# The first two weight blocks loaded and cast by column halves, and the remaining queries of batches 0 and 1 loaded ahead of batch 2

## The chip, the cores and the metric

The kernel runs on one core of one Trainium2 chip. The metric is the device time of one execution in microseconds (us). A profiled execution also gives a span, from the first to the last instruction of the program; it was about 1.8 us shorter than the time of the same execution.

In the profile the engines are PE (TensorE matmuls), PEld (its weight loads), DVE (VectorE), ACT (ScalarE), POOL (GpSimd) and SP (SyncE, whose queue issues nearly all DMAs here). The text says VectorE for DVE.

## The reference

Linear attention on 8 batches of 8 heads, 576 positions and 64 channels, followed by a two-layer network on all 4,608 rows:

```python
q_s = exp(q - max(q, -1)) / sum(..., -1)        # softmax over the channels
k_s = exp(k - max(k, 2))  / sum(..., 2)         # softmax over the positions
kv  = einsum('bhsd,bhse->bhde', k_s, v)
x   = einsum('bhsd,bhde->bhse', q_s, kv)        # -> (4608, 512)
h   = x @ w_in                                  # 512 -> 2048
g   = h * sigmoid(beta * h)
out = g @ w_out                                 # 2048 -> 512
```

## The kernel before

The rows are cut into nine slabs of 512. Slab t, for t below 8, holds the first 512 positions of batch t. The last 64 positions of each batch, the *remaining* queries, are gathered for the ninth slab. They go in pairs of batches: loaded into `QRF`, exponentiated into `EQR`, normalized, transposed by a DMA into `QTR`, and multiplied on PE by the `KVD` of their two batches.

A slab has a first pass (`x @ w_in`, then Silu on ACT) and a second (`g @ w_out`). PE interleaves the attention work of the next batch with these. The kernel gives each engine its instructions in the order of the program. The helper `add(engine, instruction, r=, w=)` derives waits from what is read and written.

Three places matter. The first is the start, where the first weight group `(c = 0)` is loaded in four blocks `m` of 128 rows by 512 columns and cast to bf16. The second is the queue order of batch loads. The third is the product with `QTR` in slab 1.

```python
def load_qrem(b):                  # two loads, rows of 64 float32 = 256 bytes
    for h in range(2):
        a = bass.AP(qt_h, (b + h) * H * S * D + SM * D, [[D, SR], [S * D, H], [1, D]])
        ...                        # SP: dma_start(QRF[i][64 * h:64 * h + 64, :, :], a)

def load(b):                       # all of it on the SP queue, in this order
    load_main("qf", qt_h, QF, b)
    load_k(b)
    load_v(b)
    if b % 2:
        load_qrem(b - 1)
# ... cut ...
def load_win(c, m=0, nm=NM):       # a block: 128 rows of 512 columns, 2 KB each
    a = bass.AP(win_h, m * 128 * DFF + 512 * c, [[DFF, 128], [128 * DFF, nm], [1, 512]])
    add(SP, lambda e: e.dma_start(STAGE[c][:, m:m + nm, :], a), w=SKEY[c][m:m + nm], ...)
# ... cut: start of slab 0 ...
out_now(0, 0, 0, ACTE)
cast_win(0, 0, DVE)                # block 0 of the first group
kv_mm(0, 2, 7, 0, D + 1)
ksum_inv(0, 7, 2, 1, D, 1)
kvd(0, 2, 7, 0)
cast_win(0, 1, DVE)                # block 1; blocks 2 and 3 are cast by POOL
out_now(0, 1, 6, ACTE)
at = by_m(0, 0, 4)                 # first-pass matmuls of columns 0:512, block by block
kv_mm(0, 3, 1, 0, D + 1)
at(0)
# ... cut: end of slab 0 ...
if t == 0:
    load(2)
    load_qrem(0)
    ...
    store(0)
    load(3)                        # contains load_qrem(2)
    continue
# ... slab 1, between the passes ...
if t == 1:
    nb = [2, 3]
    exp_qr(0)                      # ACT: EQR <- exp(QRF)
    norm_rem(0)                    # VectorE: sums, reciprocals, scaling
    tr_dma(0)                      # SP: QTR <- EQR, a transposing DMA
for b in nb:
    exp_q(b)
    ...
# the second pass of slab 1 contains the products with QTR, then batch 2's attention
```

The products with `QTR` cannot simply be put later on PE. They read the `KVD` of batches 0 and 1, and the next thing that PE does for the attention is to make the `KVD` of batch 2 in the same buffer.

The softmax here doesn't subtract the row's maximum and nothing guards it: scores larger than these inputs give would overflow.

Of the kernel before, what the change touches and what calls it, by code (L numbers as in the profile page):

```python
# [17 lines left out]
DFF = 2048  # L18
NF = DFF // 128
NM = DM // 128  # L20
# [136 lines left out]
def bass_efficient_attn_shen__then__act_swish_beta_kernel(  # L157
# [12 lines left out]
    with ExitStack() as es:  # L170
# [24 lines left out]
        WIN = sb("WIN", [128, NM, DFF], BF16)  # L195
# [20 lines left out]
        add = P.add  # L216
# [55 lines left out]
        def load_v(b, split=1, cs=None):  # L272
            load_pairs("vf", vt_h, VF, b, split, cs)

        def load(b):
# [5 lines that stand above are left out]
# [65 lines left out]
        def cast_v(b, hp, eng=POOL, part=None):  # L346
            i = b % 2
            j0, n = ((0, NG), (0, 5), (5, 4))[0 if part is None else part + 1]
            o = bass.AP(VB[i], (hp * NG + j0) * VW, [[NHP * NG * VW, 128], [VW, n], [1, 64]])
            a = bass.AP(VF[i], hp * KW + j0 * D, [[NHP * KW, 128], [64, n], [1, 64]])  # L350
            add(eng, lambda e: (e.copy if eng == ACTE else e.tensor_copy)(o, a),  # L351
                r=[("vf", i, hp), ("vone", i)],
                w=[("vb", i, hp, h) for h in ((0, 1) if part is None else (part,))])
# [211 lines left out]
        def cast_win(c, m, eng):  # L565
            add(eng, lambda e: e.tensor_copy(WIN[:, m, 512 * c:512 * c + 512], STAGE[c][:, m, :]),  # L566
                r=[SKEY[c][m]], w=[("win", c, m)])

        KB = 2

        def turn_beta():
# [36 lines left out]
        go(t_steps(0, (1,), (4,)))  # L608
        ksum(0, 0, KB)
        load_v(0, 4)  # L610
        for c in range(4):
            for m in range(0, NM, 1 if c < 2 else 2):
                load_win(c, m, 1 if c < 2 else 2)
        cast_v(0, 0)
        cast_v(0, 1)
        cast_v(0, 2, ACTE)
        cast_v(0, 3)
        cast_win(0, 2, POOL)
        cast_win(0, 3, POOL)
        cast_win(1, 0, POOL)  # L620
# [13 lines left out]
        def pass1_mm(t, f, m, bk):  # L634
            x = XT8 if t == 8 else XT[t % 2]
            rd = [("xt8", p_) for p_ in range(4)] if t == 8 else [("xt", t % 2, m)]
            n = 2 if f < 8 else 4
            l = bass.AP(WIN, m * DFF + 128 * (f // n * n) + f % n, [[NM * DFF, 128], [n, 128]])
            mm(PS[bk][:, :], l, x[:, m, :], m == 0, m == NM - 1,
               r=rd + [("win", f // 4, m)], w=[("ps", bk)], bk=bk)  # L640
            if m == NM - 1:
                add(ACTE, lambda e: e.activation(GT[:, f, :], PS[bk][:, :], ACT.Silu,  # L642
                                                 scale=BETA[:, f:f + 1]),
                    r=[("ps", bk), "beta"], w=[("gt", f)], bank=[bk])
# [17 lines left out]

        FIRST = (16, 5)
        out_now(0, 0, 0, ACTE)
        cast_win(0, 0, DVE)
        kv_mm(0, 2, 7, 0, D + 1)
        ksum_inv(0, 7, 2, 1, D, 1)
        kvd(0, 2, 7, 0)
        cast_win(0, 1, DVE)
        out_now(0, 1, 6, ACTE)  # L670
        at = by_m(0, 0, 4)
        kv_mm(0, 3, 1, 0, D + 1)
# [36 lines left out]
        def o2_evac(t, u, bk, eng=DVE):  # L709
            add(eng, lambda e: (e.copy if eng == ACTE else e.tensor_copy)(  # L710
                O2S[t % 2][:, u, :], PS[bk][:, :]),
                r=[("ps", bk)], w=[("o2", t % 2, u)], bank=[bk])
# [41 lines left out]
        for t in range(NSLAB):  # L754
            todo = []
            if t == 0:
                def kv1():
                    kv_mm(1, 1, 0, 1, D + 1)
                    ksum_inv(1, 0, 0, 2, D, VW)
                    kvd(1, 0, 0, 0, 2)  # L760

                def evacs():
                    o2_evac(0, 0, 3, DVE)
                    exp_kh(1, 3, 1, 1)
                    exp_kh(1, 3, 1, 0)
                    o2_evac(0, 1, 4, ACTE)

                todo = [(107, lambda: go(t_steps(1, (0, 1), (1,), ACTE))),
                        (112, lambda: go(t_steps(1, (2, 3), (2,), ACTE))),
                        (112.1, lambda: (scale_wout(14, 2), exp_kh(1, 2, 1, 0), exp_kh(1, 2, 1, 1))),  # L770
                        (115, lambda: kv_mm(1, 0, 0, 0, D + 1)), (117, kv1),
                        (122, lambda: out_now(1, 0, 7, DVE)),
                        (123, lambda: out_now(1, 1, 1, ACTE)), (124.5, evacs),
                        (126, lambda: go(kv_steps(1, (2,), (0,))))]
            elif t == 1:
                todo = spread(outr_steps(1), 101.5, 103) + attn_late(2)
            elif t < 7:
                todo = attn(t + 1)
            todo = sorted(todo, key=lambda x: -x[0])
            slot = [0]  # L780

            def tick():
                slot[0] += 1
                while todo and todo[-1][0] <= slot[0]:
                    todo.pop()[1]()

            if 2 <= t < 7:
                for hp in (0, 2):
                    norm_main(t + 1, hp, 2)
                    t_dma(t + 1, hp, 2)  # L790
                if t % 2 == 0:
                    norm_rem(t // 2)
                    tr_dma(t // 2)
                if t == 2:
                    load(5)
            elif t == 1:
                for hp in range(NHP):
                    cast_v(2, hp)
            if t < 2:
                slot[0] = NM * FIRST[t]  # L800
            for f in range(FIRST[t] if t < 2 else 0, NF):
                pass1_tile(t, f, tick)
            if t == 0:
                load(2)
                load_qrem(0)
                scale_wout(0)
                scale_wout(4)
                exp_q(1, 0, 2)
                norm_main(1, 0, 1)
                scale_wout(8)  # L810
                norm_main(1, 1, 1, POOL)
                exp_q(1, 2, 2)
                exp_kh(1, 0, 2, 0)
                exp_kh(1, 0, 2, 1)
                norm_main(1, 2, 1, POOL)
                norm_main(1, 3, 1)
                scale_wout(12, 2)
                for hp in range(NHP):
                    cast_v(1, hp, POOL if hp else ACTE)
                pass2_group(0, (0, 1, 2, 3), (3, 4, 5, 6), tick)  # L820
                while todo:
                    todo.pop()[1]()
                at = by_m(1, 0, FIRST[1])
                o2_evac(0, 2, 5, ACTE)
                add(ACTE, lambda e: e.activation(DUMMY[:, 2:3], WARM[:, 0:1], ACT.Silu),
                    r=["warm"], w=["dummy"])
                at(0, 0, 3)
                out_now(1, 2, 7, DVE)
                at(1, 0, 3)
                go(kv_steps(1, (3,), (0,)))  # L830
                at(0, 3)
                at(1, 3)
                out_now(1, 3, 7, DVE)
                at(2)
                at(3)
                o2_evac(0, 3, 6, DVE)
                store(0)
                load(3)
                continue
            nb = [t + 2] if t + 2 < B else []  # L840
            if t == 1:
                nb = [2, 3]
                exp_qr(0)
                norm_rem(0)
                tr_dma(0)
            for b in nb:
                exp_q(b)
                if b == 2:
                    for hp in range(2):
                        norm_main(2, hp, 1, POOL)  # L850
                    t_dma(2, 0, 2)
                if b % 2 == 1:
                    exp_qr(b // 2)
                exp_k(b, step=2)
                if b > 3:
                    for hp in range(NHP):
                        cast_v(b, hp)
                if b + 2 < B and t > 1:
                    load(b + 2)
            for u in range(4):  # L860
                if (t, u) == (8, 3):
                    last_tile(u, ((0, 384), (384, 512)), (OB[orot[0] % 2], MB[0]))
                    continue
                pass2_group(t, (u,), (OB[orot[0] % 2],), tick)
                orot[0] += 1
                if t == 1 and u == 0:
                    for hp in range(2, 4):
                        norm_main(2, hp, 1, POOL if hp == 2 else DVE)
                    t_dma(2, 2, 2)
                    for hp in range(NHP):  # L870
                        cast_v(3, hp)
                    load(4)
            while todo:
                todo.pop()[1]()
            if t < 8:
                store(t)
# [30 lines left out]
```

## Time and profile before

| quantity | value |
|---|---|
| time, median of the 6 runs beside the changed kernel | 285.24 us (284.43 to 285.64) |
| span of the profiled execution | 283.1 us |
| PE busy | 275.2 us, 97% |
| first weight matmul starts | 13.77 us |
| product with `QTR` starts | 68.08 us |

These are the page's span, its first busy rows, the granted clock and the busy share of the DMA engines in 40 slices of 7.08 us (9 is 90% or more), and the two rows of the chain that ended last.

```profile
span 283.1 us, 3884 instructions
...
PE 275.2 (97%) x1559; PEld 136.0 (48%) x1589; DVE 117.3 (41%) x218; ACT 178.6 (63%) x243; POOL 38.6 (14%) x57
...
PEclk9999999999999999999999999999999999999999
DMA  7999999998998998217980033002500030012022
...
PE 90%; ACT 4%; DMA 3%; issue 1%; DVE 1%; SPq 0%; ACTq 0%
PE PS L366 89%; ACT EK L317 2%; DMA KF<-in_k_dram 2%; DMA QTR<-EQR 2%; ACT L322 0%; SPq L249 0%; PE PS L364 0%; ACT GT L642 0%; DVE QRS L340 0%; DVE EQR L343 0%; ACT VB L351 0%; ACT EQR L322 0%; ACT XT L530 0%; ACT O2S L710 0%; DVE O2S L731 0%
```

PE is the bound, and at full clock. No faster load, cast or exponential helps unless PE was waiting for it. PE busy is a coarse guide here, because the page models where pipelined matmuls end. The better reading is the distance from one matmul's start to the next one's: a 512-column matmul takes 215 to 216 ns. I looked in the trace for distances beyond that. Excesses of about 216 ns, one in about every 50 records, I took for missing records. What remains after 13 us is small: 0.11 us at 13.77, 0.17 us at 16.98, about four of 0.1 us or somewhat more between 39 and 53, and 0.73 us at 68.08.

The lines below are of the timeline of PE: start, time from there to the end of the group, engine, line, operation, output and inputs, shape, count, and in brackets idle time before it with what ended it. First the start of the first pass:

```profile
13.77 1.02 PE L366 MATMUL PS<-XT,WIN 128*128 128x512 bf16 x4
14.63 0.38 PE L366 MATMUL PS<-QT,KVD 128*128 128x512 bf16 x1
```

Four weight matmuls start at 13.77 and the next product follows at 14.63 without a hole. And at the remaining queries:

```profile
59.15 8.36 PE L366 MATMUL PS<-WOUT,GT 128*128 128x512 bf16 x37
68.08 0.26 PE L366 MATMUL PS<-QTR,KVD 128*128 128x64 bf16 x3 [0.57 <-DMA QTR<-EQR]
```

PE has run through 37 matmuls of the second pass and then waits for `QTR`. The last start before the wait was at 67.135 us, so PE could have gone on at 67.35; it went on at 68.08.

The queue and ACT tell where `QTR` came from. The first answer is the timeline of SP, where the second number is how long the issue occupied SP; the second is that of ACT.

```profile
33.42 0.43 SPq L249 DMA_DIRECT2D QF<-in_q_dram  x1
...
41.74 4.48 SPq L266 DMA_DIRECT2D QRF<-in_q_dram  x2
...
49.30 0.43 SPq L249 DMA_DIRECT2D QF<-in_q_dram  x1
...
54.13 5.35 SPq L266 DMA_DIRECT2D QRF<-in_q_dram  x2
63.69 1.29 SPq L456 DMA_TRANSPOSE QTR<-EQR  x1
```

```profile
46.19 1.28 ACT L825 ACT_TABLE_LOAD   x1
...
48.87 5.99 ACT L642 ACTIVATE GT<-PS,BETA 128x512 bf16<-128x512 f32 x10 [1.18 <-PE PS L366]
...
61.35 0.63 ACT L322 ACTIVATE EQR<-QRF 128x512 bf16<-128x512 f32 x1
```

The remaining queries of batches 0 and 1 are issued at 41.74, behind batch 2 (its q is the issue at 33.42), and landed, by the trace, at 54.0 and 54.4. Batch 3 follows from 49.30 on, with its own remaining queries last (54.13). ACT, busy with Silu, exponentiates them only at 61.35, and the transpose is issued at 63.69. It landed at 68.03.

### The profile page before, as it was taken

What the parts mean: (1) busy time and instruction counts of PE and PEld (TensorE: products, weight loads), DVE (VectorE), ACT (ScalarE), POOL (GpSimd) and SP (SyncE); (2) the same over time, 40 slices, a digit from 0 to 9 for tenths busy, and PEclk for the clock granted to TensorE, in tenths of its full rate; (3) what the DMA queues carried; (4) which work ended last, traced back from release to release, by engine and by line L of the source; (5) the groups of instructions that cost most, each with busy time, mean ns of one, the idle gap of its engine ahead of it and who ended that gap; (6) DMA issues with size and microseconds to landing.
All of it is one profiled execution on the core that took longest, in us unless ns stands there. A gap on an engine that the chain in (4) does not pass through costs nothing.

```text
span 283.1 us, 3884 instructions
## 1 busy us (share of the span) xinstructions
PE 275.2 (97%) x1559; PEld 136.0 (48%) x1589; DVE 117.3 (41%) x218; ACT 178.6 (63%) x243; POOL 38.6 (14%) x57
## 2 busy tenths in 40 slices
PE   7899999999999999999999999999999999999995
PEld 3545454444455445544554445444544444444443
DVE  4864886029781348124841473055705300110012
ACT  5968687999968926795579636892660076017500
POOL 6522041308021032100130000000000000000000
PEclk9999999999999999999999999999999999999999
DMA  7999999998998998217980033002500030012022
GB/s 243 375 391 400 389 387 378 347 382 138 336 322 251 362 365 285 39 35 252 375 102 1 0 150 74 2 1 100 141 2 0 9 141 0 0 54 96 0 74 74
DMA packets 41466, 50.07 MB, mean 177 GB/s; under 512 B 20324, under 2 KB 28772, under 8 KB 40296
## 3 DMA queue, kind: packets, MB, share of 16 engines
q1 hardware_dynamic: 40496, 48.77, 53.7%
q10 hardware_dynamic: 952, 1.06, 1.1%
q8 instruction: 12, 0.20, 0.3%
q14 instruction: 6, 0.05, 0.0%
HBM read 36.71 MB, written 9.44 MB: 163 GB/s over the span
## 4 chain that ended last, share of the span: by engine, by line
PE 90%; ACT 4%; DMA 3%; issue 1%; DVE 1%; SPq 0%; ACTq 0%
PE PS L366 89%; ACT EK L317 2%; DMA KF<-in_k_dram 2%; DMA QTR<-EQR 2%; ACT L322 0%; SPq L249 0%; PE PS L364 0%; ACT GT L642 0%; DVE QRS L340 0%; DVE EQR L343 0%; ACT VB L351 0%; ACT EQR L322 0%; ACT XT L530 0%; ACT O2S L710 0%; DVE O2S L731 0%
## 5 line engine op out<-in xcount | busy, mean ns | idle before, releaser
L642 ACT ACTIVATE GT<-PS,BETA 128x512 bf16<-128x512 f32 x144 | 96.6, 689 | 79.0 <-PE PS L366 79.0
L366 PE MATMUL PS<-WOUT,GT 128*128 128x512 bf16 (+2 forms) x579 | 131.4, 373 | 0.7 <-issue 0.2
L366 PE MATMUL PS<-XT,WIN 128*128 128x512 bf16 x561 | 131.2, 379 | 0.5
L366 PEld LDWEIGHTS PS<-XT,WIN 128*128 128x128 bf16 x576 | 60.1, 106 | 59.3 <-POOL WIN L566 0.5
L366 PEld LDWEIGHTS PS<-WOUT,GT 128*128 128x128 bf16 x592 | 55.3, 98 | 62.0 <-DVE O2S L710 0.2
L710 DVE COPY O2S<-PS 128x512 f32<-128x512 f32 x33 | 22.7, 687 | 107.7 <-PE PS L366 107.7
L366 PE MATMUL PS<-VB,EK 128*128 128x65 bf16 (+2 forms) x306 | 35.8, 191 | 1.2 <-ACT VB L351 0.7
L351 POOL CAST VB<-VF 128x576 bf16<-128x576 f32 x30 | 22.7, 757 | 76.5 <-DMA VF<-in_v_dram 47.1
L307 ACT ACTIVATE EK<-KF 64x1152 bf16<-64x1152 f32 x24 | 27.8, 1157 | 0.4
L366 PEld LDWEIGHTS PS<-VB,EK 128*128 128x128 bf16 x306 | 22.0, 98 | 8.1 <-ACT VB L351 0.8
L332 DVE TENSOR_REDUCE QS<-EQ 128x8 f32<-128x512 bf16 (+1 forms) x22 | 20.1, 913 | 3.1 <-ACT EQ L295 2.9
L441 DVE CAST XT<-PS 128x512 bf16<-128x512 f32 x24 | 16.4, 690 | 10.9 <-PE PS L366 10.9
L295 ACT ACTIVATE EQ<-QF 128x512 bf16<-128x512 f32 x32 | 17.9, 619 | 3.0 <-DMA QF<-in_q_dram 2.8
L334 DVE TENSOR_TENSOR EQ<-EQ,QI 128x1024 bf16<-128x1024 bf16 (+1 forms) x15 | 16.9, 1128 | 0.5
L366 PE MATMUL PS<-QT,KVD 128*128 128x512 bf16 x30 | 11.4, 379 | 0.0
L317 ACT ACTIVATE EK<-KF 64x576 bf16<-64x576 f32 (+1 forms) x12 | 9.9, 839 | 1.8 <-DMA KF<-in_k_dram 1.7
L334 POOL TENSOR_TENSOR EQ<-EQ,QI 128x512 bf16<-128x512 bf16 x7 | 7.3, 1042 | 18.5 <-DVE QI L333 18.2
L403 DVE TENSOR_TENSOR KVD<-PS,RC 64x64 bf16<-64x64 f32 (+2 forms) x28 | 8.6, 308 | 1.3 <-PE PS L364 0.5
L340 DVE TENSOR_REDUCE QRS<-EQR 128x8 f32<-128x512 bf16 x4 | 2.7, 678 | 13.2 <-ACT EQR L322 13.2
L366 PE MATMUL PS<-XT 128*128 128x512 f32 x10 | 6.7, 801 | 1.5 <-DVE XT L219 1.5
L642 ACT ACT_TABLE_LOAD x5 | 6.4, 1283 | 0.1
L295 ACT ACT_TABLE_LOAD x5 | 6.4, 1283 | 0.1
(52 smaller groups left out, 77.5 us busy)
## 6 DMA issues: line engine op xcount, KB each, us to landing
out_dram<-O2S SPq DMA_DIRECT2D x8, 1024.0 KB, 4.6
KF<-in_k_dram SPq DMA_DIRECT2D x6, 1152.0 KB, 8.2
VF<-in_v_dram SPq DMA_DIRECT2D x6, 1152.0 KB, 11.4
QF<-in_q_dram SPq DMA_DIRECT2D x6, 1024.0 KB, 6.8
KF<-in_k_dram SPq DMA_DIRECT2D x8, 288.0 KB, 8.1
VF<-in_v_dram SPq DMA_DIRECT2D x8, 288.0 KB, 8.7
WST<-in_moe_w_in_dram SPq DMA_DIRECT2D x8, 256.0 KB, 7.8
O2S<-in_moe_w_in_dram SPq DMA_DIRECT2D x4, 512.0 KB, 11.9
```

Of the source, the lines that this page charges most:

```text
L295: add(ACTE, lambda e, o=o, a=a: e.activation(o, a, ACT.Exp), r=[("qf", i, hp)], w=[("eq", i, hp)])
L307: add(ACTE, lambda e, o=o, a=a: e.activation(o, a, ACT.Exp), r=[("kf", i, h) for h in hps], w=[("ek", i, h, e_) for h in hps])
L317: add(ACTE, lambda e: e.activation(o, a, ACT.Exp), r=[("kf", i, h) for h in hps], w=[("ek", i, h, e_) for h in hps])
L332: add(DVE, lambda e: e.tensor_reduce(s_, a, AX.X, ALU.add), r=ks, w=[("qs", i, hp0)])
L334: add(eng, lambda e: e.tensor_tensor(a, a, vb, ALU.mult), r=ks + [("qi", i, hp0)], w=ks)
L340: add(DVE, lambda e: e.tensor_reduce(QRS[:, :], EQR[i][:, :, :], AX.X, ALU.add), r=[("eqr", i)], w=["qrs"])
L351: add(eng, lambda e: (e.copy if eng == ACTE else e.tensor_copy)(o, a), r=[("vf", i, hp), ("vone", i)], w=[("vb", i, hp, h) for h in ((0, 1 ...
L366: add(PE, lambda e: e.matmul(o, l, r_, start=start, stop=stop), r=r, w=w, bank=[bk])
L403: add(DVE, lambda e, o=o, a=a, s_=s_: e.tensor_tensor(o, a, s_, ALU.mult), r=[("ps", bk)] + [("rc", i, h) for h in hps], w=[("kvd", i, h, ...
L441: add(eng, lambda e: (e.copy if eng == ACTE else e.tensor_copy)(XT[i][:, hp, :], PS[bk][:, :]), r=[("ps", bk)], w=[("xt", i, hp)], bank=[bk])
L642: add(ACTE, lambda e: e.activation(GT[:, f, :], PS[bk][:, :], ACT.Silu, scale=BETA[:, f:f + 1]), r=[("ps", bk), "beta"], w=[("gt", f)], ba ...
L710: add(eng, lambda e: (e.copy if eng == ACTE else e.tensor_copy)(O2S[t % 2][:, u, :], PS[bk][:, :]), r=[("ps", bk)], w=[("o2", t % 2, u)], ...
```

## The change

The change has two parts. The *halves*: blocks 0 and 1 of the first group are loaded together, 256 columns at a time, so that one load of 256 KB, as large as a block's load before, brings half of both (a *half load*). VectorE casts the left halves and POOL the right ones, to shorten the way to the first matmuls and to relieve VectorE. The *queries*: the remaining queries of batches 0 and 1 are loaded ahead of batch 2. Their exponential goes before ACT's Silu work, and their normalization and transpose into the end of slab 0, so that PE need not wait for `QTR`.

```diff
+        def load_wh(h):
+            a = bass.AP(win_h, 256 * h, [[DFF, 128], [128 * DFF, 2], [1, 256]])
+            add(SP, lambda e: e.dma_start(STAGE[0][:, 0:2, 256 * h:256 * h + 256], a),
+                w=[("wsth", h)], slot=f"winh{h}")
+
+        def cast_wh(m, h, eng):
+            c = slice(256 * h, 256 * h + 256)
+            add(eng, lambda e: e.tensor_copy(WIN[:, m, c], STAGE[0][:, m, c]),
+                r=[("wsth", h), SKEY[0][m]], w=[("winh", m, h)])
 ...
+        load_wh(0)
+        load_wh(1)
         for c in range(4):
-            for m in range(0, NM, 1 if c < 2 else 2):
+            for m in range(0 if c else 2, NM, 1 if c < 2 else 2):
                 load_win(c, m, 1 if c < 2 else 2)
 ...
         cast_v(0, 3)
+        cast_wh(0, 1, POOL)
+        cast_wh(1, 1, POOL)
         cast_win(0, 2, POOL)
 ...
-               r=rd + [("win", f // 4, m)], w=[("ps", bk)], bk=bk)
+               r=rd + [("winh", m, f // 2) if f < 4 and m < 2 else ("win", f // 4, m)],
+               w=[("ps", bk)], bk=bk)
 ...
-        cast_win(0, 0, DVE)
+        cast_wh(0, 0, DVE)
 ...
-        cast_win(0, 1, DVE)
+        cast_wh(1, 0, DVE)
 ...
             if t == 0:
+                load_qrem(0)
                 load(2)
-                load_qrem(0)
 ...
                 o2_evac(0, 2, 5, ACTE)
+                exp_qr(0)
 ...
                 o2_evac(0, 3, 6, DVE)
+                norm_rem(0)
                 store(0)
                 load(3)
+                tr_dma(0)
                 continue
 ...
             if t == 1:
                 nb = [2, 3]
-                exp_qr(0)
-                norm_rem(0)
-                tr_dma(0)
```

## The prediction

> **What bounds the kernel.** The page's busy table: PE 275.2 of 283.1 us (97%), granted clock 1.0. The chain of waits runs 89% through PE's matmul line. PE waits for k, v and softmax until 12.87 us and hardly stops after 13.8, so only idle PE time can be won. From the timeline's starts (a 512-column matmul every 215 ns) I find after 13 us, besides an excess of 215 ns about every 50 records, taken for a missing record: 0.11 us at 13.77 (first weight matmul; its block landed at 13.17, VectorE cast it 13.20 to 13.63), 0.17 us at 16.98 (fourth x tile, evacuated until 16.83), about four of 0.1 us between 39 and 53, and 0.73 us at 68.08, where the remaining-query product waits for the transposed load QTR (waits view: 1.1 us for the weight load, 0.6 for the matmul). The change aims at the first and the last: at most 0.9 us.
>
> **Part 1, the halves.** Same bytes; rows of 1 KB instead of 2 KB. Packets took about 46 ns per 1,024 B at the start and 75 ns per 2,048 B in the weight loads: 512 KB should take 1.5 instead of 1.2 us over 16 engines, an estimate. The Trainium skill, "DMA: Bandwidth & Descriptors", section "Why small descriptors are slow (HBM only)", names a fixed cost per packet; the trace agrees (22 against 27 B/ns). So the first half lands near 13.3, the second near 14.0, later weights up to 0.3 us later. VectorE casts halves (estimate 0.25 us, from 0.42 for a whole); POOL must cast the others (estimate 0.35 us, from 0.61 to 0.80) before columns 256 to 511 can be used, which PE wants at 14.1. I expect the 0.11 us stall to go and one of 0.1 to 0.4 us, on POOL, before the third matmul: net -0.1 to +0.3, centre +0.1. The 0.17 us at 16.98 stays.
>
> **Part 2, remaining queries.** They landed at 54.0 and 54.4 behind batch 2; now near 45.5. Their exp (0.61 us, ACT) then runs near 46.2, before the Silu table load, after which ACT waited 1.18 us for PE: free, unless they land after 47. Sums, scaling and transpose issue, at 62.0 to 63.7 before, come at about 49 on VectorE and 59.5 on the queue. The transpose took 4.35 us to land at 68.03 (median 3.0): batch 3's own last piece landed at 67.47, and it still stands behind that batch. I expect QTR at 67.0 to 67.9, against a need at 67.35: saves 0.2 to 0.73 us, centre 0.45. Lighter ACT and VectorE in slab 1's second pass gain nothing.
>
> **Sum.** +0.1 - 0.45 = -0.35 us; the runs before spread 0.9 us, their median at the top. Predicted 284.8 us, 8 in 10 within 283.9 to 285.6. Faster by over 2%: 0.5%; within 2%: 99%; slower: 0.5%.
>
> **What shows it.** Right: the remaining exp near 46 without a DMA wait, slab 1's first Silu still near 48.9; QTR wait under 0.5 us; a PE weight-load wait on POOL's cast at 14; span 282.3 to 283.2. Part 2 wrong if the transpose lands at 68 or later (queue order decides, not issue time). Part 1 wrong if weight matmuls start clearly before 13.6 or PE runs through.
>
> **What would break it.** Remaining queries landing after 47: ACT holds back slab 1's Silu, PE loses up to 1 us. 256-byte rows slowing batch 1's last k and v (needed near 45.7, landed 43.9). A stall that timed runs have and the profile does not.

## The result

| | before | after |
|---|---|---|
| time, median of 6 | 285.24 us (284.43 to 285.64) | 285.24 us (284.78 to 286.22) |
| span of the profiled execution | 283.1 us | 283.1 us |
| first and third weight matmul start | 13.77, 14.20 us | 13.76, 14.53 us |
| remaining queries land | 54.0, 54.4 us | 44.7, 45.4 us |
| their exponential starts | 61.35 us | 46.30 us |
| transpose issued | 63.69 us | 59.11 us |
| `QTR` lands | 68.03 us | 67.98 us |
| PE ready for `QTR` | 67.35 us | 67.58 us |
| product with `QTR` starts | 68.08 us | 68.03 us |

The ratio of the changed kernel's time to that of before is 1.0011, with a 95% interval of 0.9987 to 1.0034: the same. "PE ready" is worked out: the start of the last matmul before the product with `QTR`, plus 216 ns.

The page of the changed kernel, the same parts as before:

```profile
span 283.1 us, 3887 instructions
...
PE 275.7 (97%) x1559; PEld 136.1 (48%) x1589; DVE 117.6 (42%) x218; ACT 178.7 (63%) x243; POOL 39.1 (14%) x59
...
PE 89%; DMA 6%; SPq 2%; ACT 1%; issue 1%; POOL 0%; DVE 0%
PE PS L366 89%; DMA QTR<-EQR 3%; DMA WST<-in_moe_w_in_dram 3%; SPq L259 1%; ACT EK L317 0%; SPq L249 0%; PE PS L364 0%; ACT GT L657 0%; ACT XT L530 0%; ACT O2S L725 0%; SPq L571 0%; POOL WIN L576 0%; DVE O2S L746 0%
```

The span is the same. The chain now passes through the transpose for 3% of the span, which is its 8.9 us from issue to landing: it was issued early and landed late.

The start of the first pass, first PE, then POOL:

```profile
13.76 0.59 PE L366 MATMUL PS<-XT,WIN 128*128 128x512 bf16 x2
14.53 0.61 PE L366 MATMUL PS<-XT,WIN 128*128 128x512 bf16 x2 [0.17 <-POOL WIN L576]
14.97 0.38 PE L366 MATMUL PS<-QT,KVD 128*128 128x512 bf16 x1
```

```profile
14.07 0.86 POOL L576 CAST WIN<-WST 128x256 bf16<-128x256 f32 x2 [0.80 <-DMA WST<-in_moe_w_in_dram]
```

PE starts two weight matmuls at 13.76 and then waits for POOL. From start to start the hole is 0.33 us, although the bracket counts 0.17, because the second matmul still counts as running. So the product that started at 14.63 before starts at 14.97 now. The right halves landed at 14.02, POOL's first cast ran 0.40 us from 14.07, and PE went on at 14.53.

At the remaining queries:

```profile
59.38 8.37 PE L366 MATMUL PS<-WOUT,GT 128*128 128x512 bf16 x37
68.03 0.26 PE L366 MATMUL PS<-QTR,KVD 128*128 128x64 bf16 x3 [0.29 <-DMA QTR<-EQR]
```

PE comes about 0.23 us later than before (59.38 against 59.15), waits less (0.29 against 0.57 in brackets, 0.45 against 0.73 from start to start) and goes on at nearly the same moment. The queue and ACT:

```profile
33.05 4.24 SPq L266 DMA_DIRECT2D QRF<-in_q_dram  x2
37.33 2.68 SPq L249 DMA_DIRECT2D QF<-in_q_dram  x1
...
52.18 6.88 SPq L266 DMA_DIRECT2D QRF<-in_q_dram  x2
59.11 4.69 SPq L456 DMA_TRANSPOSE QTR<-EQR  x1
```

```profile
46.30 0.63 ACT L322 ACTIVATE EQR<-QRF 128x512 bf16<-128x512 f32 x1
46.95 1.28 ACT L841 ACT_TABLE_LOAD   x1
...
49.09 5.99 ACT L657 ACTIVATE GT<-PS,BETA 128x512 bf16<-128x512 f32 x10 [0.64 <-PE PS L366]
```

Everything in front of the transpose moved forward as meant. The queries (33.05) are issued ahead of batch 2 (37.33), ACT exponentiates them without waiting for a load, and the first Silu of slab 1 still starts when PE delivers (49.09). Yet the transpose (59.11) stands behind all of batch 3 in the queue, its remaining queries (52.18) last, and lands 0.56 us after the last piece of it (67.42), as it did before (67.47 and 68.03).

### The profile page after: what moved, and what is told of

It reads as the page before. It is cut to its first block, busy times and chain, and to the rows that moved or that the text cites. A ratio compares the mean times of both kernels' runs of the same rounds, so it can differ in the third digit from the quotient of the medians.

```text
span 283.1 us, 3887 instructions
## 1 busy us (share of the span) xinstructions
PE 275.7 (97%) x1559; PEld 136.1 (48%) x1589; DVE 117.6 (42%) x218; ACT 178.7 (63%) x243; POOL 39.1 (14%) x59
## 4 chain that ended last, share of the span: by engine, by line
PE 89%; DMA 6%; SPq 2%; ACT 1%; issue 1%; POOL 0%; DVE 0%
PE PS L366 89%; DMA QTR<-EQR 3%; DMA WST<-in_moe_w_in_dram 3%; SPq L259 1%; ACT EK L317 0%; SPq L249 0%; PE PS L364 0%; ACT GT L657 0%; ACT XT L530 0%; ACT O2S L725 0%; SPq L571 0%; POOL WIN L576 0%; DVE O2S L746 0%
## 5 line engine op out<-in xcount | busy, mean ns | idle before, releaser
L424 DVE RECIPROCAL RC<-PS 128x4 f32<-128x4 f32 (+2 forms) x9 | 1.6, 177 | 9.5 <-PE PS L366 9.4
```

## The experiments

The theory to be tested has two parts. The *queue-order theory*: `QTR` lands half a microsecond after whatever load was issued ahead of the transpose, no matter when the transpose was issued. The *absorption theory*: PE must wait for that moment anyway, so what is lost or won in front of it does not reach the time. The rival is that the two parts simply add: the halves lose about what the queries win. A second rival, for kernels that remove the wait, is that the gain is given back at a later wait.

The kernels of one group were timed on the same chip, in rounds with the same runs of the kernel before. Edits are given against the changed kernel.

### First group

**Queries alone.** The halves are taken out (loads and casts of whole blocks, as before).

```diff
-        load_wh(0)
-        load_wh(1)
-            for m in range(0 if c else 2, NM, 1 if c < 2 else 2):
+            for m in range(0, NM, 1 if c < 2 else 2):
-        cast_wh(0, 1, POOL)
-        cast_wh(1, 1, POOL)
-        cast_wh(0, 0, DVE)
+        cast_win(0, 0, DVE)
-        cast_wh(1, 0, DVE)
+        cast_win(0, 1, DVE)
 ... (the matmuls read the whole blocks again)
```

> Second part of the change alone (whole blocks as before). Absorption theory: QTR still lands at 67.8 to 68.2 us, because it stands behind batch 3's loads; PE, now without the 0.33 us stall at 14.5, reaches it near 67.4 and waits 0.6 to 0.75 us there; span within 0.1 us of before. Rival, additive parts: the halves cost 0.3 and the earlier queries save as much, so that this one alone ends 0.3 to 0.45 us earlier, QTR wait under 0.45.

Measured: 285.31 us (ratio 1.0011, 0.9998 to 1.0024), span 283.3. The timeline of PE:

```profile
59.05 8.37 PE L366 MATMUL PS<-WOUT,GT 128*128 128x512 bf16 x37
68.25 0.26 PE L366 MATMUL PS<-QTR,KVD 128*128 128x64 bf16 x3 [0.84 <-DMA QTR<-EQR]
```

PE is ready 0.33 us earlier than in the changed kernel (67.25) and waits longer: 1.00 us from start to start, more than the 0.6 to 0.75 that I expected, since `QTR` landed at 68.20. Batch 3's last piece had landed at 67.67. Additivity falls: without the halves nothing was won, though the rival expected 0.3 to 0.45 us, and the interval allows 0.06 us at most.

**Halves alone.** The queries are put back to where they were.

```diff
-                load_qrem(0)
                 load(2)
+                load_qrem(0)
-                exp_qr(0)                      # after o2_evac(0, 2, 5, ACTE)
-                norm_rem(0)
                 store(0)
                 load(3)
-                tr_dma(0)
+                exp_qr(0)                      # back in slab 1
+                norm_rem(0)
+                tr_dma(0)
```

> First part alone (queries as before). Absorption theory: PE stalls 0.3 to 0.35 us before the third weight matmul near 14.5 on POOL's cast, then waits only about 0.45 us for QTR, which lands near 68.0; span within 0.1 us of before. Additive rival: the span grows by 0.25 to 0.35 us, QTR landing later by the same.

Measured: 284.86 us (ratio 0.9997, 0.9982 to 1.0012). The 0.32 us hole before the third weight matmul is there again (on POOL, at 14.70). In the profiled execution the span was 283.9, with `QTR` landing at 68.80 and a wait of 0.99 us. That looks like the additive rival's span, but not for its reason: PE was ready at 67.86 and waited for a landing that came 0.55 us after batch 3's last piece, at 68.25. The times do not show a loss, but the interval reaches 0.34 us, so this run alone does not exclude the rival; queries alone does. The span of one execution moves with the landing by some tenths, as the table below makes plain.

**Transpose first.**

```diff
                 store(0)
-                load(3)
                 tr_dma(0)
+                load(3)
```

> The changed kernel with the transpose of the remaining queries issued ahead of batch 3's loads. Queue-order theory: issued near 51, it lands between 54 and 58, the QTR wait is gone, PE passes that point near 67.6 instead of 68.03 and the span falls by 0.4 to 0.5 us against the changed kernel (0.3 to 0.5 against before). Rival, the gain is given back: batch 3 now starts about 1.3 us later and a later PE wait (second slab's Silu or batch 3's exp) takes it; span as before, with a new gap after 68.

Measured: 284.69 us (ratio 0.9992, 0.9977 to 1.0006), span 283.7. `QTR` landed at 58.73, 0.56 us after the store in front of it, so the queue-order theory holds, and the `QTR` wait is gone. The rival is right about the time, at a place that it did not name. The timeline of PE:

```profile
68.18 0.25 PE L366 MATMUL PS<-QTR,KVD 128*128 128x64 bf16 x3
...
72.23 0.39 PE L366 MATMUL PS<-QT,KVD 128*128 128x512 bf16 x1 [0.36 <-DMA QT<-EQ]
```

PE now waits 0.53 us from start to start for `QT`, the transposed queries of batch 2. That transpose was issued at 66.10, behind batch 3, which started later here and landed at 70.51. The transpose landed at 72.18, 1.67 us behind batch 3: the half microsecond holds for `QTR`, not for every transpose. The wait for the queue moved on by one transpose. In this execution PE also came to the `QTR` product late (68.18). It had lost some 0.5 us near 26 and 29 us; the first load of the second-pass weights landed at 28.03 against 26.75 in the changed kernel.

**Whole loads, half casts.** The two blocks are loaded whole, but still cast in halves by both engines.

```diff
-        load_wh(0)
-        load_wh(1)
-            for m in range(0 if c else 2, NM, 1 if c < 2 else 2):
+            for m in range(0, NM, 1 if c < 2 else 2):
-                r=[("wsth", h), SKEY[0][m]], w=[("winh", m, h)])
+                r=[SKEY[0][m]], w=[("winh", m, h)])
```

> The changed kernel, with its casts in halves but the two blocks loaded whole again (2 KB rows), so that POOL's first half needs only the first block, landing near 13.2. If the late second half (landing 14.0) makes the 0.33 us stall, PE starts the weight matmuls near 13.7 and runs through the first four. If POOL's slow cast makes it, a stall of about 0.15 us or more remains before the third. Absorption theory: the span does not change either way (within 0.1 us), and the QTR wait grows to 0.7 us or more.

Measured: 285.36 us (ratio 1.001, 0.9997 to 1.0023), span 283.7. The four first weight matmuls run through, from the timeline of PE and of POOL:

```profile
13.83 1.02 PE L366 MATMUL PS<-XT,WIN 128*128 128x512 bf16 x4
14.69 0.38 PE L366 MATMUL PS<-QT,KVD 128*128 128x512 bf16 x1
```

```profile
13.35 1.06 POOL L576 CAST WIN<-WST 128x256 bf16<-128x256 f32 x2 [0.39 <-DMA WST<-in_moe_w_in_dram]
```

POOL starts its right half at 13.35, when block 0 has landed (13.30), and is done in time although this cast took 0.52 us, longer than in the changed kernel (0.40). So it was the landing of the right halves, one load later, and not POOL's speed, that made the hole. The time did not fall: `QTR` landed at 68.56, and PE's wait grew to 1.16 us. This is absorption again.

### Second group

**Transpose behind v.** Only batch 3's remaining queries are put behind the transpose.

```diff
-                load(3)
+                load(3, False)       # q, k, v; load() is given this switch
                 tr_dma(0)
+                load_qrem(2)
```

> The changed kernel with the transpose issued behind batch 3's q, k and v, but ahead of its remaining queries (256-byte rows). If those two small-row loads are what QTR stands behind, it lands 0.5 to 1 us earlier relative to batch 3's v (near or before v's landing), the QTR wait of PE falls under 0.2 us and the span by 0.3 to 0.5 us. If v and k (the bulk) decide, QTR still lands after v's landing (near 67 to 68), the wait stays at 0.3 us or more, and the span is within 0.2 us of the changed kernel.

Measured: 284.29 us (ratio 0.9977, 0.9964 to 0.9989), span 282.5. The timeline of PE, and of SP:

```profile
59.27 8.36 PE L366 MATMUL PS<-WOUT,GT 128*128 128x512 bf16 x37
67.48 0.25 PE L366 MATMUL PS<-QTR,KVD 128*128 128x64 bf16 x3
```

```profile
52.34 0.80 SPq L259 DMA_DIRECT2D VF<-in_v_dram  x1
53.18 6.78 SPq L456 DMA_TRANSPOSE QTR<-EQR  x1
60.01 2.85 SPq L266 DMA_DIRECT2D QRF<-in_q_dram  x2
```

No wait is left: 37 matmuls, and the product with `QTR` follows at 67.48. `QTR` landed at 66.79, 0.53 us after batch 3's v (66.26). The two loads with 256-byte rows landed at 67.46 and 67.95 instead. So those 256 KB ahead of the transpose were enough to make PE wait. The span fell by 0.56 us against the changed kernel, a little more than the 0.3 to 0.5 that I had expected. This is the first kernel whose interval lies under 1; its five times lie within 0.23 us, and those of the kernel before in the same rounds within 0.92.

**Three deferrals.** To leave no queue in front of either transpose, the transpose goes first, and batch 3's v and remaining queries are issued only after batch 2's transposes; their exponential goes behind the rest of batch 3's.

```diff
-                load(3)
                 tr_dma(0)
+                load_main("qf", qt_h, QF, 3)
+                load_k(3)
 ...
-                if b % 2 == 1:
+                if b % 2 == 1 and b != 3:
                     exp_qr(b // 2)
 ...
                     t_dma(2, 2, 2)
+                    load_v(3)
+                    load_qrem(2)
+                    exp_qr(1)
```

> The changed kernel with the transpose ahead of batch 3, and batch 3's v and remaining queries issued only after batch 2's two transposes, so that neither QTR nor QT has a queue before it. Queue theory (the stream of loads decides, PE's arrival does not): no PE wait for QTR nor QT; PE reaches the QTR product near 67.6 us (with the 0.33 us stall at 14.5 still there) and the span is that plus 215.05, about 282.4 to 282.8. Times 0.3 to 0.7 us under the kernel before, and less spread. Rival, gain given back again: a new gap of 0.3 us or more after 68, as for QT in the run with the transpose first (candidates: batch 3's v cast on POOL near 77, the first Silu of slab 2), span 283.1 or more.

The second has this and whole blocks (the edit of the first experiment):

> The same deferral without the halves. With nothing left to absorb it, the 0.33 us stall of the halves must now show: PE reaches the QTR product 0.2 to 0.4 us earlier than with them (near 67.3), span 282.2 to 282.6, time 0.6 to 1.0 us under the kernel before (ratio 0.9965 to 0.998). If the head's time is absorbed elsewhere, the span equals that of the deferral with halves within 0.1 us.

The third has this and whole loads with half casts:

> The deferral with whole loads and casts in halves. The first weight matmuls run through without a gap (it was 0.06 to 0.11 without half casts): span 0.05 to 0.1 us under the deferral without halves, if the loads before land alike; more likely hidden in how the first loads scatter (the first of them landed 0.3 us apart between runs). Time 0.6 to 1.1 us under the kernel before.

Measured: 285.26, 285.26 and 284.96 us (ratios 1.0014, 1.0014 and 0.9998; intervals 1.0001 to 1.0027, 1.0 to 1.0028 and 0.9985 to 1.001). The rival holds in all three. `QTR` and `QT` are no longer waited for, but there is a new hole near 79. From start to start it reads 1.03, 0.85 and 0.69 us; 0.22 us of each is a missing record, for the traces of the other kernels show an excess of 0.22 us at the same matmul. So 0.81, 0.63 and 0.47 us were lost, by which the rest of the span grew too (table below). The expected gain in time, 0.3 us or more in each, was missed. The first hole, from the timelines of PE and ACT:

```profile
78.15 0.23 PE L366 MATMUL PS<-VB,EK 128*128 128x65 bf16 x2
79.24 0.19 PE L366 MATMUL PS<-VB,EK 128*128 128x65 bf16 x1 [0.87 <-ACT GT L657]
```

```profile
76.33 0.63 ACT L322 ACTIVATE EQR<-QRF 128x512 bf16<-128x512 f32 x1 [1.11 <-DMA QRF<-in_q_dram]
...
78.27 2.63 ACT L657 ACTIVATE GT<-PS,BETA 128x512 bf16<-128x512 f32 x4
```

My own edit made it. The remaining queries of batch 3 now landed at 76.25, ACT waited 1.11 us for them, and the table load and Silu of slab 2 came that much later. The halves could not be priced here either: without them PE was ready at 67.54 instead of 67.59, because in that execution the first whole block landed late (13.46) and PE lost 0.25 us before the first weight matmul, and 0.31 us before that.

### Third group

The transpose goes between batch 3's k and v, with the three kinds of first loads.

```diff
-                load(3)
+                load_main("qf", qt_h, QF, 3)
+                load_k(3)
                 tr_dma(0)
+                load_v(3)
+                load_qrem(2)
```

With halves:

> The changed kernel with the transpose issued between batch 3's k and v (halves kept). Queue-order theory: QTR lands right after k, 63 to 64.5 us, no PE wait for it; batch 2's QT still lands in time (as in the run with the transpose behind v), so PE has no gap after 68 and the span is PE's arrival (67.4 to 67.7) plus 215.05: 282.4 to 282.8, time about 0.6 us under before. If the wait moves on to QT or the Silu as in the earlier two reorderings, a new gap shows after 68 and the span is 283 or more.

With whole blocks:

> The same transpose place without the halves. With the QTR wait gone nothing absorbs the halves' 0.33 us stall: this one's stall after 13.6 is under 0.25 us in all and its time 0.1 to 0.4 us under the run with halves of the same rounds; span 282.1 to 282.5. If the halves cost nothing, the two times agree within 0.1 us.

With whole loads and half casts:

> The same transpose place, blocks loaded whole and cast in halves on two engines. No gap between the first and the fourth weight matmul; time as the run without halves, or up to 0.1 us under it, and 0.1 to 0.4 us under the run with half loads. This is meant as the version that beats both kernels: ratio to before about 0.9965 to 0.998.

Measured: 284.46, 284.25 and 284.34 us (ratios 0.9974, 0.9969 and 0.9974; intervals 0.9956 to 0.9992, 0.9951 to 0.9986 and 0.9955 to 0.9993). All three are ahead of the kernel before, by a gain far inside the 2% that count as the same here but clear of 1 by the intervals, and none waits for `QTR`. The timeline of PE in the third:

```profile
13.68 1.02 PE L366 MATMUL PS<-XT,WIN 128*128 128x512 bf16 x4
14.54 0.38 PE L366 MATMUL PS<-QT,KVD 128*128 128x512 bf16 x1
```

```profile
58.95 8.37 PE L366 MATMUL PS<-WOUT,GT 128*128 128x512 bf16 x37
67.15 0.25 PE L366 MATMUL PS<-QTR,KVD 128*128 128x64 bf16 x3
```

Its span of 282.2 us is the shortest of all; the best time is that of whole blocks. So the transpose between k and v with whole blocks, 284.25 us, is the best version; it beats the kernel before by 0.31% (ratio 0.9969). It was not timed in the same rounds as the changed kernel, whose ratio to the kernel before was 1.0011. The hole before the third weight matmul was 0.34 us with half loads and absent in the other two. In times, half loads came out 0.21 us behind whole blocks and 0.12 behind whole loads with half casts, by the medians. The sign is the expected one, but the intervals overlap, so the price of the halves in time stays unproven. Nor do the traces price it: PE was ready for `QTR` at 67.42 with half loads and at 67.41 with whole blocks, where the first weight matmul had started 0.33 us later (13.93 against 13.60). In the profiled execution with halves `QTR` landed 2.07 us after k instead of 0.5, and PE lost 0.53 us for `QT` at 71.47. Why it landed late in that one execution is open.

### All executions in one table

The landing of the DMA issued ahead of the transpose, `QTR`'s landing, PE's readiness, the start of the product with `QTR`, and what remains of the span from there, in us, from each trace:

| kernel | transpose issued | piece ahead landed | `QTR` landed | PE ready | product starts | rest of the span |
|---|---|---|---|---|---|---|
| before | 63.69 | 67.47 | 68.03 | 67.35 | 68.08 | 215.05 |
| changed | 59.11 | 67.42 | 67.98 | 67.58 | 68.03 | 215.06 |
| queries alone | 59.88 | 67.67 | 68.20 | 67.25 | 68.25 | 215.05 |
| halves alone | 64.20 | 68.25 | 68.80 | 67.86 | 68.85 | 215.05 |
| whole loads, half casts | 60.16 | 68.00 | 68.56 | 67.44 | 68.60 | 215.06 |
| transpose first | 51.39 | 58.17 | 58.73 | 68.18 | 68.18 | 215.56 |
| transpose behind v | 53.18 | 66.26 | 66.79 | 67.48 | 67.48 | 215.04 |
| three deferrals, halves | 50.81 | 57.67 | 58.17 | 67.59 | 67.59 | 215.85 |
| three deferrals, whole blocks | 50.76 | 57.15 | 57.66 | 67.54 | 67.54 | 215.68 |
| three deferrals, half casts | 50.40 | 57.14 | 57.64 | 67.17 | 67.17 | 215.52 |
| between k and v, halves | 52.53 | 63.44 | 65.50 | 67.42 | 67.42 | 215.57 |
| between k and v, whole blocks | 52.42 | 63.41 | 63.90 | 67.41 | 67.41 | 215.06 |
| between k and v, half casts | 52.30 | 63.57 | 64.10 | 67.15 | 67.15 | 215.05 |

In the first five rows the transpose is issued at any time between 59.11 and 64.20 and always lands 0.53 to 0.57 us after the last piece of batch 3. PE is ready at any time between 67.25 and 67.86 and always goes on about 0.05 us after that landing. The rest of the span is then 215.05 or 215.06 us. So up to that point the span is the landing's affair alone. That is also why the first group's spans of 283.3, 283.9 and 283.7 us missed the "within 0.1 us" that I had expected of them: the landing itself lay between 67.98 and 68.80. What moves it is open. The DMA row of the page, 90% or more from 7 to 64 us, suggests a reading: the engines are still working through what the queue holds, so an earlier issue only waits longer in it. Where the rest is longer, there is a later hole (0.53 us for `QT` in transpose first and in between k and v with halves, the loss near 79 in the deferrals).

## Why the prediction was right or wrong

The time, 285.24 us, lies in the predicted range of 283.9 to 285.6, and "within 2%" was right. The predicted centre of 284.8 was 0.44 us low. That the time lay in the range is owed to the width of the range: it also holds the kernel before, and none of the forecast saving of 0.35 us came.

**What bounds the kernel.** Right. Only holes on PE count, and the span followed them to within hundredths.

**Part 1, the halves.** The stall came as described, on POOL before the third matmul, at 0.33 us (expected 0.1 to 0.4). It was also there, at 0.32 to 0.34 us, in all five other executions with half loads, and in none of the seven with whole loads. The right halves landed at 14.02, as predicted, but partly for another reason than the one given. I had put up to 0.3 us on the 1 KB rows. That rested on a packet time for 2,048 bytes that no packet of the traces has: they show 46 ns for 1,024 bytes and 84 ns for 2,048 (medians), so a fixed cost is there, but 512 KB over 16 engines would cost only 0.13 us more, an estimate from these medians. From the last v landing to the second weight landing took 1.35 to 1.76 us in the seven executions with whole blocks (mean 1.56) and 1.44 to 1.70 in the six with halves (mean 1.52). A cost of the short rows does not show, though one of 0.13 us could hide in this spread; in the changed kernel v itself landed 0.16 us later than before. The cost of the halves is the order of the data. The third matmul needs only block 0, which a whole load brings first, while the half loads bring its right half second. The half casts did bring something: VectorE's cast took 0.29 us instead of 0.43, and the first weight matmul started 0.46 to 0.53 us after its block or half had landed in the nine executions with half casts, against 0.59 to 0.66 us in the four with whole casts. The 0.11 us stall before it was gone in the changed kernel, as forecast, but because PE arrived 0.10 us later; in the other five executions with half loads 0.10 to 0.29 us remained.

**Part 2, the remaining queries.** Their landing near 45.5, the exponential near 46 that costs ACT nothing, and the transpose issue near 59.5 were all right (45.4, 46.30, 59.11). The step that failed is "I expect QTR at 67.0 to 67.9, against a need at 67.35: saves 0.2 to 0.73 us". It landed at 67.98, 0.05 us earlier than before, when PE was ready at 67.58. The prediction had noticed that the transpose "still stands behind that batch" and yet gave the earlier issue half the gain. The order in the queue was the whole of it: the saving came only when the transpose was issued ahead of part of batch 3. The forecast "QTR wait under 0.5 us" was met at 0.45 by luck: the wait is 0.28 us shorter than before because PE came 0.23 us later, not because `QTR` came earlier.

**The sum.** "+0.1 - 0.45" treats the terms as independent. They meet at one point: PE goes on when both its own work and `QTR` are there, so the later of the two counts. The halves' loss of 0.33 us was inside PE's wait for `QTR`, and so was the gain of taking them out. Shown by queries alone, halves alone and whole loads with half casts: in the first five rows of the table PE's readiness differs by up to 0.61 us, and each time PE went on with the landing.

**What would break it.** None of the three named dangers came: the queries landed in time, batch 1's v landed at 44.12 against 43.92 without a new hole, and the runs' times agree with their profiles. The spread of the runs before, which I had noted, fits a span that hangs on one landing, but only one run of each kernel has a trace, and the times of the third version between k and v, which does not wait for `QTR`, spread by 0.88 us too. So this is not shown.

## What to carry to other kernels

Before moving work earlier, find what the waited-for DMA stands behind in its queue. If it lands a constant time after the piece ahead of it, as `QTR` did, issuing it sooner gains nothing, and reordering two issues can. Savings in front of a wait do not add to savings at the wait: the later of the two arrivals counts, so take the wait away first, and look for the next transpose or activation that comes to stand in its place. And when a load is cut in pieces, cut it so that the first piece holds all that the first consumer needs.

## What the Trainium skill lacked or had wrong

- "DMA: Bandwidth & Descriptors", section "Queues, rings and completion order", says that descriptors are consumed in ring order on each DMA engine. The traces agree as far as they go: the DMAs issued by SP landed in the order of issue in all 13. What the page lacks is how long after the piece ahead of it a transposing DMA lands (an estimate from the page's transpose bandwidth aside). Here one of 128 KB (128 rows of 512 bf16) with loads or a store ahead of it on the same queue landed 0.49 to 0.57 us after the piece ahead in 12 of 13 executions (2.07 in one), whether it was issued 4 or 14 us before it landed.
- The same page, section "Issuing engines are not separate DMA queues", calls the sequencer's time to initiate a DMA usually small relative to the DMA itself. It was not small here with other DMAs ahead: the issue of that transpose occupied SP for 1.29 of its 4.35 us from issue to landing in the kernel before, 4.69 of 8.87 us in the changed one and 6.78 of 13.61 us behind v, and the issue of a load of 1,152 KB took 6.51 us. In the transpose behind v the next issue on SP started at 60.01, after those 6.78 us. What decides between 1.29 and 6.78 us is not shown.
- The same page, section "Why small descriptors are slow (HBM only)", explains a fixed cost per packet. Packet records agree (medians of 46 ns for 1,024 bytes, 84 ns for 2,048 and 164 ns for 4,096), but the landings do not show it: 512 KB of weights landed 1.52 us (mean of 6) after v with 1 KB rows and 1.56 us (mean of 7) with 2 KB rows. The page gives no packet times for rows of these sizes.
- "Perfetto Trace Analysis" warns in its opening that matmul busy time is a poor measure of distance to the roofline, because matmuls are pipelined. PE's idle time before the product with `QTR` reads 0.57 us, while the starts of the matmuls are 0.73 us further apart than their 216 ns. The skill knows the start-to-start distance of matmuls in a stream, but no page measures a stall of PE by what exceeds it.
